# Order of a range check, a key transpose, a product block, a weight difference and three loads in a gated recurrence with a maxout layer

## The chip, the cores and the metric

The kernel runs on one core of one Trainium2 chip. The metric is the device time of one launch in microseconds. A profiled execution records every instruction of the five engines with its start and duration: TensorE (PE, with its weight loads as PEld), VectorE (DVE), ScalarE (ACT), GpSimd (POOL) and SyncE (SP), which here only issues DMAs. Each engine works through its own instructions in the order of the program and waits on semaphores.

## What is computed

There are two stages. The first is a recurrence for each of 4 batches and 8 heads over 768 steps, with states of 48 x 48. The second is a layer on the 3072 tokens of 384 features that the first one gives.

```python
f = 1.0 / (1.0 + np.exp(-f_logit))
for t in range(S):
    state = f[:, :, t, :, None] * state + np.einsum('bhd,bhe->bhde', k[:, :, t], v[:, :, t])
    y[:, :, t] = np.einsum('bhd,bhde->bhe', q[:, :, t], state)
# x is y with the heads of a token side by side
h = np.maximum(np.maximum(x @ w1, x @ w2), x @ w3)     # 384 -> 768
return h @ w_out                                        # 768 -> 384
```

The weights come as 64-bit floats. The kernel rounds them to 32 bits by integer and float operations on their two halves, and checks that their sizes lie in a range for which this rounding holds.

## The kernel before

**Units and groups.** The work is cut in 24 units of 128 tokens (64 steps of two batches). Four units make a group; group g is the layer's work on units 4g to 4g+3. A unit's part of the recurrence is: `sigmoids` (ACT, L305), `scan` (DVE: running products of the gates, L324), `after` (k times these, `kh`, L334), `before` (q times others, `qh`, L345), `carry` (L354), `keys` (transposes of `kh` into `ks`, on PE for units 4 and 5, and by 32 x 32 blocks on DVE from unit 6, L361 and L372), `pairs` (products of `kh` and `qh`, L389), `values` (L403), `sums` (L424) and `finish` (L496). `values` ends with a copy of one element on ACT, `seen` (L422), and the products of `finish` (L504) wait for it. From unit 6 on f, k and q are loaded two units at a time, in blocks of 32 rows: 8 DMAs for each of the three (L183), all issued by SP. `kt` and `qt` are the blocks transposed by DVE (L296), and from unit 6 the products `kh` (L340) and `qh` (L351) are made by POOL.

**Order.** The order is written out by hand (L992 onward). One loop over u from 4 to 23 (L1071) does, for each u, `pairs(u)`, `values(u-1)`, `sums(u-1)`, `finish(u-1)` and the preparation of unit u+1. Between them it calls `fill(ns)` (L967), which takes as many pieces of the layer's work from a generator as cost `ns` by an estimate. The generators yield after each block of products, so where a block stands in a generator decides which blocks lie between two steps of a unit. At u = 8 group 1 is put in the queue, at u = 12 group 2, and so on; the last group runs after the loop.

**The first group** (`ffn_first`, L797) runs plain products while the weights come in. Near its end it places w2 - w1 and w3 - w1 in another layout by DMAs inside the chip's memory (`place`, L454: 10 DMAs for each of the two, and 10 for a product of weights, w_lin). Then sums of placed weights are made (`mix_in`, L844, on POOL), and differences of w_out's quarters (`mix`, L588, on POOL). `mix(1)` overwrites a quarter of w_out, so the first group's products with w_out must have read it.

**Later groups** (`inputs_by_pairs`, L869) compute the two products of the layer's inputs by a scheme with fewer products: for each n of three, blocks named `start`, `plain`, `fifth`, `sixth`, `seventh`, `third` and `fourth`. Each call of `into` is two products of 256 columns (L881), which the profile shows as four records. Blocks accumulate in two kinds of PSUM banks: A[n] from a pool of two (named `p`) and B[n] from a pool of two (named `tr`). `plain(n)` fills B[n], and ACT copies it out (L889); `fifth(n)` writes B[n] anew, so it waits for that copy. `start(n)` fills A[n], copied by L895 into one buffer that POOL's `join(n)` (L899) reads; `sixth(n)` adds to A[n], copied by L909, and `seventh(n)` adds to it again, after that copy. `sixth` and `fifth` take sums of x made by POOL (`sums_of_x`, L856, five operations at L865); these need rows of x moved by `pack` (L519, DMAs at L524).

**The range check** of a piece of the weights (`check_range`, L272) is three steps on ACT: a size (L278) and two sums (L280), one piece for each unit from u = 10 on, and the rest after the loop.

**Names in the trace.** `tr` and `p` are the PSUM banks, `rest_bits` and `top_bits` also serve as buffers of the layer, `placed` holds the placed weights, `a` and `y` are the recurrence's banks. SPq means an issue by SP.

Of the kernel before, what the change touches and what calls it, by code (L numbers as in the profile page):

```python
# [55 lines left out]
def kernel(  # L56
# [15 lines left out]
    NU = B // 2 * (S // C)  # L72
# [5 lines left out]
    GRP = 4  # L78
# [11 lines left out]
    def fast():  # L90
        ctx = ExitStack()
        with ctx:
# [58 lines left out]
            BY_ROWS = 6  # L151
# [5 lines left out]
            one = (nc.sync, nc.sync)  # L157
# [590 lines left out]
            def store_late():  # L748
                while late:
                    store(*late.pop(0))  # L750
# [46 lines left out]
            def ffn_first(xT):  # L797
                hm = new_hm()
                steps = [(j, slice(n * HALF, (n + 1) * HALF)) for n in range(2) for j in range(J_HALF)]
                steps += [(j, slice(0, TOK)) for j in range(J_HALF, NJ)]  # L800
                n_step = 0
                for j, t in steps:
                    w = t.stop - t.start
                    for i in (1, 2):
                        p = yield from product(xT, j, i, t)
                        if i == 1:
                            nc.scalar.copy(hm[:, j, t], p)
                        else:
                            nc.vector.scalar_tensor_tensor(hm[:, j, t], hm[:, j, t], 0.0, p, op0=ALU.max, op1=ALU.max)
                        round_to(ROUNDED[n_step])  # L810
                        load_weights(2, rounded[0] - 1)
                        yield (1 if w == TOK else NK) * w * COLUMN
                        n_step += 1
                        if n_step in TURNED:
                            yield from turn(TURNED[n_step])
                for a in range(NK):
                    if a < 2:
                        for n in range(2 * NK + 2):
                            place(placed[a].bitcast(FP32), w_in[a + 1], n)
                    for cost in linear(a):  # L820
                        round_to(rounded[0] + 1)
                        yield cost
                for n in range(2 * NK + 2):
                    place(w_lin, w_nat, n)
                made = iter([lambda n=n: mix_in(n) for n in range(4)] + [lambda: mix(0)])
                for i in range(GRP):
                    for n, cost in enumerate(outputs(hm, xT, i)):
                        if i or n:
                            next(made, lambda: None)()
                        if i == GRP - 1 and n == 1 and 1 in packed:  # L830
                            sums_of_x(1)
                        if i == GRP - 1 and n == 2:
                            for k in range(1, 4):
                                mix(k)
                        yield cost

# [32 lines left out]
            def inputs_by_pairs(g, hm, xT):  # L869
# [37 lines left out]
                def sixth(n):  # L907
                    into(A[n], n, s2, t2)
                    nc.scalar.copy(out(n, 1), two(A[n]))  # L909
                    yield COST  # L910
# [29 lines left out]
                yield from plain(0)  # L940
                join(0)
                store_late()
                yield from sixth(0)
                yield from fifth(0)
                for n in range(1, NJ // 2):
                    yield from plain(n)
                    yield from seventh(n - 1)
                    yield from start(n)
                    join(n)
                    yield from third(n - 1)  # L950
                    yield from fifth(n)
                    yield from sixth(n)
                    yield from fourth(n - 1)
# [38 lines left out]
            with tc.manual_schedule():  # L992
# [78 lines left out]
                for u in range(GRP, NU):  # L1071
                    n = u + 1
                    part = EARLY if u < 2 * GRP else PART
                    if n == BY_ROWS:
                        scan(n)
                    fill(part)
                    keys(u)
                    keys_by_blocks(u, 2)
                    room_of_unit = room_of_pairs()
                    if u > GRP:  # L1080
                        values(u - 1)
                        sums(u - 1, room_of_unit)
                    pairs(u, room_of_unit)
                    if u > GRP:
                        finish(u - 1, xT)
                        if u % GRP == 3:
                            pack(0, 2, xT)
                        elif u % GRP == 0:
                            pack(3, 3, xT)
                    if u % GRP == 0:  # L1090
                        if u > GRP:
                            packed[u // GRP - 1] = xT
                            pending.append(ffn(u // GRP - 1, xT))
                        xT = x_tiles[u // GRP % 2]

                    if u + 2 <= BY_ROWS:
                        load(u + 2)
                    if BY_ROWS <= u + 3 < NU and u % 2:
                        load(u + 3, one, "fkq" if u % GRP == 1 else "f")
                    if u + 2 < NU:  # L1100
                        load_v(u + 2)
                    keys_by_blocks(u, 3)
                    if n < NU:
                        if n < BY_ROWS:
                            sigmoids(n)
                        if n != BY_ROWS:
                            scan(n)
                    check_range(u - CHECKS, 0)
                    fill(part)
                    if n < NU:  # L1110
                        after(n)
                        before(n)
                    fill(part)
                    if BY_ROWS < u + 2 < NU and u % GRP == 0:
                        load(u + 2, one, "k")
                    if n < NU:
                        carry(n)
                    else:
                        values(u)
                    check_range(u - CHECKS, 1)  # L1120
                    fill(part)
                    if BY_ROWS < u + 2 < NU and u % GRP == 0:
                        load(u + 2, one, "q")
                    if n == NU:
                        finish(u, xT)
                        pack(3, 3, xT, both)
                        packed[u // GRP] = xT
                    keys_by_blocks(n, 0)
                    fill(part - 1000 if u < 2 * GRP else part)
                    keys_by_blocks(n, 1)  # L1130
                    check_range(u - CHECKS, 2)
                    if u + 2 >= CHECKS:
                        check_load(u + 2 - CHECKS)
                    if BY_ROWS <= u + 2 < NU:
                        sigmoids(u + 2)
                fill(PART)
                pending.append(ffn(NU // GRP - 1, xT))
# [267 lines left out]
```

## Time and profile before

| what | us |
|---|---|
| median of 3 runs (lowest, highest) | 415.52 (415.32, 416.43) |
| the profiled execution's own time | 416.13 |
| its span, first to last instruction | 414.4 |
| PE busy in the span | 393.5 |
| DVE busy | 295.1 |
| POOL busy | 246.0 |
| ACT busy | 180.4 |

The span is the time from the first instruction to the last; what is left of the execution's time lies outside. Busy times are sums over the whole span, and the limits change on the way: weights arrive until some 60 us, the first group of the layer runs to 119 us, and groups 1 to 5 take the rest, group 5 without any unit beside it. In lines of the timeline the columns are the start in us, the duration, engine, source line, operation, what is written and read, the shapes and the number of records put together, and in brackets the engine's idle time before it and what ended that. A wait on several semaphores is put down to the one that came last. The granted TensorE clock is full over the whole span but its end (0.999 in the mean).

### The profile page before, as it was taken

The numbers are of one execution on the slowest core, as the hardware profiler recorded it, in microseconds if no ns is written. First come the engines' busy times: TensorE is split into PE (matmuls) and PEld (weight loads), VectorE is DVE, ScalarE is ACT, GpSimd is POOL, SyncE is SP. The second block draws the span as 40 slices with busy tenths as digits, with TensorE's granted clock in tenths as the row PEclk, the third lists the DMA queues.
The fourth block names the chain that finished last, engine by engine and source line by source line (L and its number), as shares of the span: only waits on it lengthen the run. The fifth ranks groups of instructions, "written<-read, shape, count | busy, mean of one in ns | idle before, by whom it ended". The sixth has DMA issues, their size and how long they took to land.

```text
span 414.4 us, 11516 instructions
## 1 busy us (share of the span) xinstructions
PE 393.5 (95%) x4598; PEld 331.8 (80%) x4598; DVE 295.1 (71%) x569; ACT 180.4 (44%) x430; POOL 246.0 (59%) x270
## 2 busy tenths in 40 slices
PE   5988999999999989999999999999999999999995
PEld 4766765556667878998889988899988889988994
DVE  6997896997785899898899997998995550002600
ACT  2488786421223522335532345532445424586110
POOL 2189694830969777567495296577377860435700
PEclk9999999999999999999999999999999999999999
DMA  8999886676356766277645276735374003542002
GB/s 168 238 271 272 246 228 90 85 139 161 84 103 99 122 108 124 57 96 114 114 123 109 43 112 85 148 87 89 60 144 110 2 17 88 133 133 72 0 21 62
DMA packets 181562, 47.21 MB, mean 114 GB/s; under 512 B 160448, under 2 KB 179200, under 8 KB 181504
## 3 DMA queue, kind: packets, MB, share of 16 engines
q1 hardware_dynamic: 178032, 45.62, 54.1%
q10 hardware_dynamic: 3472, 0.81, 0.9%
q8 instruction: 37, 0.61, 0.6%
q14 instruction: 21, 0.17, 0.1%
HBM read 37.75 MB, written 4.72 MB: 102 GB/s over the span
## 4 chain that ended last, share of the span: by engine, by line
PE 74%; SPq 6%; POOL 5%; DVE 5%; ACT 4%; issue 2%; DMA 2%; POOLq 0%
PE p L881 15%; PE p L636 14%; PE tr L881 12%; PE tr L636 10%; PE p L542 7%; PE p L568 3%; PE p L787 3%; PE y L415 2%; SPq L164 2%; SPq L174 2%; DVE ks L382 2%; PE y L504 2%; PE a L396 2%; PE a L433 2%; POOL w_in L258 1%
## 5 line engine op out<-in xcount | busy, mean ns | idle before, releaser
L382 DVE STREAM_TRANSPOSE ks<-kh 32x128 f32<-32x128 f32 x256 | 77.4, 302 | 13.4 <-POOL kh L340 9.4
L881 PE MATMUL tr<-xT,placed 128*128 128x256 f32 x300 | 71.5, 383 | 1.1 <-ACT hm L889 1.1
L881 PEld LDWEIGHTS tr<-xT,placed 128*128 128x128 f32 x300 | 56.0, 190 | 10.4 <-ACT hm L889 2.6
L881 PE MATMUL p<-xT,placed 128*128 128x256 f32 x180 | 44.8, 380 | 1.1 <-POOL xT L865 0.8
L339 POOL COPY ends<-r 128x8 f32<-128x8 f32 x24 | 8.8, 366 | 51.1 <-DVE r L329 51.1
L881 PEld LDWEIGHTS p<-xT,placed 128*128 128x128 f32 x180 | 33.9, 190 | 6.4 <-POOL xT L865 1.2
L542 PE MATMUL p<-xT,w_in 128*128 128x256 f32 (+1 forms) x108 | 34.0, 459 | 3.4 <-POOL w_in L756 1.9
L329 DVE TENSOR_TENSOR_SCAN r<-gate,from_one 128x520 f32<-128x520 f32 x24 | 32.5, 1354 | 6.1 <-ACT gate L308 2.8
L340 POOL TENSOR_TENSOR kh<-kt,r 128x512 f32<-128x512 f32 x18 | 30.9, 1715 | 7.6 <-DVE kt L296 7.6
L511 ACT COPY xT<-y 64x256 f32<-64x256 f32 (+1 forms) x60 | 22.1, 368 | 23.2 <-PE y L504 22.5
L347 DVE TENSOR_TENSOR_SCAN prod<-gate,from_inv 128x520 f32<-128x520 f32 x24 | 31.5, 1312 | 0.0
L608 POOL TENSOR_TENSOR w_in<-hm 128x256 f32<-128x256 f32 x15 | 11.1, 739 | 32.2 <-DVE hm L932 29.4
L644 DVE TENSOR_TENSOR o<-tr,w_in 128x384 f32<-128x384 f32 (+1 forms) x11 | 5.7, 521 | 34.3 <-PE tr L636 29.8
L881 PE MATMUL p<-w_in,placed 128*128 128x256 f32 x120 | 30.0, 379 | 0.0
L542 PEld LDWEIGHTS p<-xT,w_in 128*128 128x128 f32 x108 | 19.5, 190 | 12.6 <-issue 6.0
L924 DVE TENSOR_TENSOR hm<-tr,hm 128x512 f32<-128x512 f32 x15 | 10.3, 684 | 23.1 <-ACT raw L280 17.2
L258 POOL TENSOR_TENSOR w_in<-top_bits,rest_bits 128x384 uint32<-128x384 uint32 x18 | 21.9, 1223 | 7.2 <-DVE top_bits L252 3.8
L636 PE MATMUL p<-w_in,hm 128*128 128x192 f32 x120 | 25.3, 334 | 0.6 <-ACT w_in L641 0.6
L641 ACT COPY w_in<-p 128x384 f32<-128x384 f32 x15 | 7.2, 478 | 42.1 <-PE p L636 42.1
L280 ACT ACTIVATE raw<-top_bits 128x384 f32<-128x384 f32 x48 | 25.2, 526 | 0.4
L881 PEld LDWEIGHTS p<-w_in,placed 128*128 128x128 f32 x120 | 22.8, 190 | 3.1
L636 PE MATMUL tr<-w_out,w_in 128*128 128x192 f32 x120 | 24.4, 326 | 0.0
(156 smaller groups left out, 913.7 us busy)
## 6 DMA issues: line engine op xcount, KB each, us to landing
raw<-in_moe_w_dram SPq DMA_DIRECT2D x24, 384.0 KB, 4.3
v_ld<-in_v_dram SPq DMA_DIRECT2D x48, 96.0 KB, 3.3
placed<-in_moe_w_dram SPq DMA_DIRECT2D x12, 384.0 KB, 5.7
out_dram<-o SPq DMA_DIRECT2D x46, 96.0 KB, 2.2
placed<-in_moe_w_out_dram SPq DMA_DIRECT2D x6, 384.0 KB, 5.4
f_ld<-in_f_logit_dram SPq DMA_DIRECT2D x36, 64.0 KB, 2.6
k_ld<-in_k_dram SPq DMA_DIRECT2D x36, 64.0 KB, 2.5
q_ld<-in_q_dram SPq DMA_DIRECT2D x36, 64.0 KB, 2.5
```

Source lines behind the costliest of these rows:

```text
L258: nc.gpsimd.tensor_tensor(dst, by(top), by(rest), op=ALU.add)
L280: nc.scalar.activation(over, size, AF.Relu, scale=(-1 / HI_MIN, 1.0)[step - 1], bias=(1.0, -HI_END * (1 - 2.0 ** -24))[step - 1], accum_ou ...
L329: nc.vector.tensor_tensor_scan(r[:, 0:LEN][:, ::-1], flat(gate)[:, ::-1], flat(from_one)[:, ::-1], 1.0, op0=ALU.mult, op1=ALU.max)
L340: (nc.vector if u < BY_ROWS else nc.gpsimd).tensor_tensor(kh.rearrange("p h a t -> p a h t"), kt, by_batch(r[:, 1:LEN + 1].rearrange("p (x ...
L347: nc.vector.tensor_tensor_scan(flat(prod), flat(gate_tiles[u % 2]), flat(from_inv[u % 2]), 1.0, op0=ALU.mult, op1=ALU.max)
L382: nc.vector.transpose(ks[n * 32:(n + 1) * 32, :, par, e0:e0 + 32], kh[p0:p0 + 32, :, a, t0:t0 + 32])
L511: nc.scalar.copy(xT[o, :, t0 + a * C:t0 + (a + 1) * C], y[i, a, 0:HP * C].rearrange("p (h t) -> p h t", h=HP))
L542: nc.tensor.matmul(p if w < TOK else p.rearrange("p (two t) -> p two t", two=2), lhsT=w_in[i][:, kt, j * 128:(j + 1) * 128], rhs=x[:, t.st ...
L568: nc.tensor.matmul(p[:, 0:DM], lhsT=lhsT, rhs=rhs, start=(n == 0), stop=(n == NJ + NK - 1))
L636: nc.tensor.matmul(b[:, p * HD:(p + 1) * HD], lhsT=x, rhs=w, start=id(b) not in begun, stop=True, skip_group_check=True)
L787: nc.tensor.matmul(p[:, 0:DM], lhsT=w_in[0][:, a, j * 128:(j + 1) * 128], rhs=w_out[:, j, :], start=(j == 0), stop=(j == NJ - 1))
L881: nc.tensor.matmul(b[:, j * HALF:(j + 1) * HALF], lhsT=w[:, (2 * n + j) * 128:(2 * n + j + 1) * 128], rhs=x, start=begin and j == 0, stop= ...
```

## The change

Five edits, in the order of the diff:

- `mix(1)` is called before `sums_of_x(1)` in the first group's last outputs, and no longer behind it with `mix(2)` and `mix(3)`.
- `plain(1)` is yielded right behind `join(0)` and the late stores, before `sixth(0)` and `fifth(0)`; for n = 1 it is left out of its old place behind `fifth(0)`.
- `keys(u)` is called behind `values(u-1)` and `sums(u-1)`. It does anything for units 4 and 5 alone, and for unit 4 no `values` stands there.
- The loads of units 8 and 9 (both in one load, 24 DMAs): at u = 5 they are left out. At u = 6 f is loaded ahead of v(8), and k and q behind the third `fill` of the unit, which is behind the second placing in SP's order. `sigmoids(8)` is done at u = 7 ahead of `scan(8)`, and not at the end of u = 6.
- The first step of the range check, `check_range(u - 10, 0)`, stands behind the second `fill` of a unit and `after` and `before`, and not ahead of that `fill`.

DVE's instructions keep their order. On PE the four transposes of unit 5 and the blocks of `plain(1)` change places; on POOL one operation moves; on ACT L278, one L889 in each group, `seen` of unit 4 and the sigmoid of unit 8; on SP 24 loads.

```diff
-                        if i == GRP - 1 and n == 1 and 1 in packed:
-                            sums_of_x(1)
+                        if i == GRP - 1 and n == 1:
+                            mix(1)
+                            if 1 in packed:
+                                sums_of_x(1)
                         if i == GRP - 1 and n == 2:
-                            for k in range(1, 4):
+                            for k in range(2, 4):
                                 mix(k)
...
                 yield from plain(0)
                 join(0)
                 store_late()
+                yield from plain(1)
                 yield from sixth(0)
                 yield from fifth(0)
                 for n in range(1, NJ // 2):
-                    yield from plain(n)
+                    if n > 1:
+                        yield from plain(n)
                     yield from seventh(n - 1)
...
                     fill(part)
-                    keys(u)
                     keys_by_blocks(u, 2)
                     room_of_unit = room_of_pairs()
                     if u > GRP:
                         values(u - 1)
                         sums(u - 1, room_of_unit)
+                    keys(u)
                     pairs(u, room_of_unit)
...
-                    if BY_ROWS <= u + 3 < NU and u % 2:
+                    if u == BY_ROWS:
+                        load(u + 2, one, "f")
+                    elif u + 1 != BY_ROWS and BY_ROWS <= u + 3 < NU and u % 2:
                         load(u + 3, one, "fkq" if u % GRP == 1 else "f")
                     if u + 2 < NU:
                         load_v(u + 2)
                     keys_by_blocks(u, 3)
                     if n < NU:
-                        if n < BY_ROWS:
+                        if n < BY_ROWS or n == BY_ROWS + 2:
                             sigmoids(n)
                         if n != BY_ROWS:
                             scan(n)
-                    check_range(u - CHECKS, 0)
                     fill(part)
                     if n < NU:
                         after(n)
                         before(n)
+                    check_range(u - CHECKS, 0)
                     fill(part)
                     if BY_ROWS < u + 2 < NU and u % GRP == 0:
                         load(u + 2, one, "k")
+                    if u == BY_ROWS:
+                        load(u + 2, one, "kq")
...
-                    if BY_ROWS <= u + 2 < NU:
+                    if BY_ROWS <= u + 2 < NU and u != BY_ROWS:
                         sigmoids(u + 2)
```

`BY_ROWS` is 6, `GRP` is 4, `NU` is 24, `CHECKS` is 10, and n is u + 1 in the unit loop.

## Prediction

> **What bounds the kernel now.** I read the busy shares, then TensorE's own waits, then the timeline around each wait. The busy shares:
>
> ```profile
> PE 393.5 (95%) x4598; PEld 331.8 (80%) x4598; DVE 295.1 (71%) x569; ACT 180.4 (44%) x430; POOL 246.0 (59%) x270
> ```
>
> TensorE (PE) is busy for 95% of 414.4 us; only its waits, and what moves them, can give time. Those that matter here (waiting engine and line <- releaser: total us, times, longest):
>
> ```profile
> PE y L504 <- ACT seen L422: 2.2, 2, 1.5
> ...
> PE tr L881 <- ACT hm L889: 1.1, 3, 0.4
> PE p L881 <- POOL xT L865: 0.8, 1, 0.8
> ```
>
> By place these fall in two parts: a filling part up to 163 us, with five waits at 124.77 (0.82), 133.94 (0.27, on ScalarE's L895), 138.20 (0.33), 155.58 (1.53) and 163.41 (0.69); and a steady part in which PE is bound by itself but for three waits of 0.38 at 188.63, 247.56 and 306.49. Before the first of them PE is gapless from 80 to 120 us.
>
> The timeline says what the filling part hangs on (start, us, instruction, [idle before <- releaser]):
>
> ```profile
> 131.86 0.71 DVE L296 STREAM_TRANSPOSE kt<-k_ld 128x512 f32<-128x512 f32 x1 [4.43 <-DMA q_ld<-in_q_dram]
> ...
> 136.17 0.71 DVE L296 STREAM_TRANSPOSE qt<-q_ld 128x512 f32<-128x512 f32 x1 [1.81 <-DMA out_dram<-o]
> ...
> 136.96 1.18 POOL L351 TENSOR_TENSOR qh<-qt,prod 128x512 f32<-128x512 f32 x1 [1.47 <-DVE qt L296]
> ...
> 138.20 0.69 PE L396 MATMUL a<-qh,kh 48*64 48x64 f32 x32 [0.33 <-POOL qh L351]
> ```
>
> VectorE (DVE) idles 4.43 us for unit 10's k and 1.81 us for its q; q gives `qt`, `qt` gives `qh` on POOL, and `qh` releases `pairs(10)` at 138.20. From 136.17 DVE has work without a break until 163.4 (145 to 165 us: 19.11 of 20 us busy), and it ends the waits at 155.58 (a copy queued behind one that waits for DVE) and 163.41. So q of unit 10 sets when PE leaves the filling part. That q comes when SP gets to it. SP's queue:
>
> ```profile
> 71.02 5.32 SPq L183 DMA_DIRECT2D f_ld<-in_f_logit_dram  x8
> ...
> 87.21 1.32 SPq L458 DMA_DIRECT2D placed<-w_in  x2
> ...
> 95.24 1.84 SPq L458 DMA_DIRECT2D placed<-w_in  x2
> ...
> 129.86 4.15 SPq L183 DMA_DIRECT2D q_ld<-in_q_dram  x8
> ```
>
> SP issues end to end from 52 to 136 us, some 0.5 us for each DMA; it is an issue bound, without a wait of note.
>
> **What the skill says.** The Trainium skill, "DMA: Bandwidth & Descriptors", section "Issuing engines are not separate DMA queues", calls the sequencer's time to initiate a DMA usually small beside the DMA. Here it is not: 0.49 us each, back to back, is what makes q late. "PSUM — Partial Sum Buffer", section "Engine vs sequencer instructions": the queues of ScalarE, VectorE and GpSimd are strict FIFO, and matmuls start in program order. The trace agrees: the 0.14 us copy `seen` (L422) stands at 67.99 behind a 0.59 us copy that nobody waits for. "TensorE: Matmul & The Clock Gate", section "Single matmul latency", gives a single warm matmul a constant of some 166 ns beside its columns, which only a stream of them hides; the trace agrees in kind: a wait shown as 0.38 moves the next start by 0.53 (246.16 to 247.56 is 1.40, where the same four records elsewhere take 0.87), and the block after a wait lasts 1.13 in place of 1.03. So such a wait costs 0.53 + 0.10 = 0.63 us.
>
> **The change part by part.** Durations are of the profiled execution (span 414.4, 416.13 us in all, 0.6 above the median of 415.52); differences are carried to the median.
>
> 1. *Loads of units 8 and 9 behind the placing.* 24 DMAs leave 71.02 and go to two places. All they pass is on SP: 4 DMAs of v and 20 of placing. Nothing is added, so from 102.33 on SP's queue is the same in order and, as far as issue bounds it, in time. In between: v(7) at 71.0, first placing 72.4 to 78.8 (1.32 + 5.06), f 78.8 to 84.1, v(8) to 85.5, second placing 85.6 to 92.6, k to 96.8, q to 101.9. The sources are ready: the last of w2 - w1 ends on POOL at 61.8, of w3 - w1 on DVE at 67.75, and the raw words under both targets are read by 72.9. POOL's L850 waits 10.86 us for the second placing and starts at 102.67; it would start some 9.6 us earlier, at 93. That frees no PE: PE has no gap there. What is late instead: q of unit 8 lands at 101.9 + 2.5 = 104.4 (median landing of such a load 2.5), where `qt(8)` ran at 102.11. DVE then idled 2.99 us at 105.78 for `kh(8)`, which came late behind L850; now `kh(8)` is made at 101.1 and `qt(8)` ends at 105.1. `qh(8)` ends at 106.3, before 106.89; `pairs(8)` starts at 108.18. Cover 1.9 us (1.4 after part 2's gain); beyond that each us late would stall PE, which could still lose 2 us before 138.20. Cost 0. `sigmoids(8)` follows the copies that end at 96.68 on ScalarE, so the 0.62 us ends at 97.3; `gate(8)` ran at 97.59. Cost 0.
> 2. *Keys of unit 5 behind values and sums of 4.* `seen` goes ahead of the `ks` copy: it starts at 67.52 rather than 67.99, and L504, which stood for 0.71, starts 0.47 earlier. Four transposes only change places. Gain 0.47 at 68 us.
> 3. *mix(1) ahead of the five sums of x.* One L592 of 1.40 us moves into POOL's 3.74 us of idle before the first sum (123.18, held by the xT transfer). The products that read w_out ended near 117.2, so it doesn't wait. The sums end when they did, `join(0)` (L899) ends 1.47 earlier. If that idle were gone, the sums would be 1.40 later.
> 4. *plain(1) ahead of sixth(0).* Same 22 products and same bank count. In group 1 it puts 1.73 us of PE in front of the product that waits for POOL's sums: wait 0.82 (0.98 by starts) goes; with part 3 the 0.27 at 133.94 (0.43 by starts) nearly goes. Gain 1.4 at 134 us. The second bank of `tr` is free: in group 2 the addition that reads it ends at 183.6, and plain(1) would start after 187.
> 5. *Range check's first step later.* Read with part 4 in the steady part, where this stands (ScalarE, then PE, in group 3):
>
> ```profile
> 246.48 0.56 ACT L278 ACTIVATE top_bits<-raw 128x384 f32<-128x384 f32 x1
> 246.94 0.57 ACT L889 COPY hm<-tr 128x512 f32<-128x512 f32 x1
> 247.40 0.59 ACT L909 COPY hm<-p 128x512 f32<-128x512 f32 x1
> ```
>
> ```profile
> 246.16 1.03 PE L881 MATMUL p<-xT,placed 128*128 128x256 f32 x4
> 247.56 2.64 PE L881 MATMUL tr<-xT,placed 128*128 128x256 f32 x11 [0.38 <-ACT hm L889]
> ```
>
> fifth(0) may only write the bank when L889 has read it; one block of 0.87 covers that, and L278 pushes the copy past it. After the change fifth(0) has three blocks of cover. What is late next: seventh(0) must wait for L909, with fifth(0) alone as cover. ScalarE's order becomes L889, L889, L278, L909. Counted from the end of plain(1): L889 0.26 to 0.84 (a copy starts 0.26 behind its block, as 361.61 to 361.87 in the last group), L278 0.74 to 1.30, L909 1.20 to 1.79, PE at 1.83 in place of 1.73. That is a loss of 0.10 + 0.10 for a gain of 0.63: 0.43 net by this count; 0.37 if the copy starts 0.06 later. I take 0.4, three times: 1.2 us. Bounds per group: 0.53 (L278 costs nothing) and 0 (L909 as late as L889 was). In the last group L278 was not in the way (0.02 stall at 362.50): 0.
>
> **The sum.** Parts 2 to 4 bring PE to `pairs(10)` 1.9 us sooner, but q(10) lands when it did, DVE's 27 us behind it are in the same order, and PE waits 0.33 + 1.9 there. They give 0. Part 5: 3 x 0.4 = 1.2. Prediction 415.52 - 1.2 = 414.3 us.
>
> **Rivals.**
> - *The front gain lives.* SP's stretch has single issues of 1.0 to 1.5 us at 73.8, 83.3 and 95.9, some 2.5 us over their 0.5; if the new order avoids them, q(10) comes sooner and PE can follow by up to 1.9. Against: the number of DMAs is the same, and such issues recur every 10 to 19 DMAs. 415.5 - 1.2 - 1.9 = 412.4.
> - *The wait only changes hands.* seventh(0) waits as long for L909 as fifth(0) did for L889: 415.5. For it: one block of cover and L278 still ahead. Against: 0.43 more lateness is needed than I can count.
> - *SP slips, slower.* A load behind placing waits for its semaphore, the eighth DMA before it; 4.2 us of issue cover it, while placings land in up to 3.7 at the median. If that or an unlucky issue delays SP before q(10), every us goes one for one to the end. At the price of the longest single issue seen since 50 us (3.0): 415.5 - 1.2 + 3.0 = 417.3; it decides from 2.5 us.
>
> **Chances.** Mine 0.52, front gain 0.18, changed hands 0.15, slip 0.15. My own range is 413.6 to 415.0 (part 5 between 0.5 and 1.6 in all, q(10) within 0.4). Over all cases 412.3 to 416.6: it cuts the far half of the first rival and most of the slip. 0.3% is 1.25 us, about what a measurement here can tell from no change; my case lies on that edge, half of it counts as faster: 0.18 + 0.26 = 0.44 faster, 0.41 within, 0.15 slower.
>
> **What would show it.** Right: no PE wait at 124.77 and none on L889 in groups 2 to 4, small ones on L909; L850 near 93; the wait before `pairs(10)` near 2.2 and its start near 138.2. Wrong: `pairs(10)` moved by over 0.5, waits on L909 of 0.3 or more, or PE stalled at `pairs(8)`.

## The result, and the profile after

The changed kernel takes 413.75 us in the median of 20 runs (411.67 to 416.40), the kernel before 415.47 us in 20 runs beside it (413.06 to 416.66). The ratio is 0.9966, with a 95% interval of 0.9950 to 0.9982: 1.4 us less, between 0.7 and 2.1. Predicted were 414.3 us.

The profiled execution of the changed kernel took 413.13 us with a span of 411.4 us, 3.0 us less than that of before. The two profiles so differ by about twice as much as the runs do (1.4 us by the ratio, 1.7 by the medians), and the experiments have to say which part of the 3.0 us belongs to the change. In the changed kernel the lines from L832 to L942 have moved down by two: L881 is now L883, L889 is L891, L909 is L911.

The busy shares of the page after:

```profile
PE 392.9 (96%) x4598; PEld 331.9 (81%) x4598; DVE 294.6 (72%) x569; ACT 180.8 (44%) x430; POOL 245.7 (60%) x270
```

PE's busy time is the same within 0.6 us; what went is idle time. PE's waits after (engine, line <- releaser: total us, times, longest):

```profile
PE y L504 <- ACT seen L422: 1.5, 1, 1.5
PE a L396 <- POOL qh L351: 0.8, 1, 0.8
...
PE p L636 <- DVE hm L933: 0.7, 1, 0.7
```

The three waits on L889 have no successor, neither on L891 nor on L911. The wait for `xT` at 124.77, the one for `rest_bits` at 133.94 and the first of the two for `seen` are gone; the one ahead of `pairs(10)` has grown from 0.33 to 0.83 us, and the two behind it are as they were (1.53 and 0.69 before). The timeline there, DVE, POOL and PE:

```profile
134.46 0.71 DVE L296 STREAM_TRANSPOSE qt<-q_ld 128x512 f32<-128x512 f32 x1 [2.39 <-DMA out_dram<-o]
...
135.25 1.18 POOL L351 TENSOR_TENSOR qh<-qt,prod 128x512 f32<-128x512 f32 x1 [2.20 <-PE y L415]
...
136.48 0.69 PE L396 MATMUL a<-qh,kh 48*64 48x64 f32 x32 [0.83 <-POOL qh L351]
```

The chain from q by `qt` and `qh` to `pairs(10)` is the same, but all of it stands 1.7 us earlier. (The profile puts the wait of `qh` down to PE's L415, which ends within 0.03 us of `qt` here; in e6 below L415 ends 4.4 us ahead of `qh`, and the time from q's landing to `pairs(10)` is the same.) So does q in SP's queue, which is issued from 128.14 us where it was from 129.86:

```profile
78.11 5.78 SPq L183 DMA_DIRECT2D f_ld<-in_f_logit_dram  x8
...
128.14 4.15 SPq L183 DMA_DIRECT2D q_ld<-in_q_dram  x8
```

In the steady part, group 3, ScalarE and then PE:

```profile
245.94 0.59 ACT L891 COPY hm<-tr 128x512 f32<-128x512 f32 x1 [1.02 <-PE tr L883]
246.42 0.57 ACT L278 ACTIVATE top_bits<-raw 128x384 f32<-128x384 f32 x1
246.88 0.58 ACT L911 COPY hm<-p 128x512 f32<-128x512 f32 x1
```

```profile
246.60 1.03 PE L883 MATMUL tr<-xT,placed 128*128 128x256 f32 x4
247.61 1.10 PE L883 MATMUL p<-w_in,placed 128*128 128x256 f32 x4
```

The order on ScalarE is the predicted one: L891, L278, L911. fifth(0) starts at 246.60 without a wait; seventh(0), at 247.61, comes 1.01 us behind it where 0.87 is its natural distance. That is 0.14 late, and the block behind it is another 0.07 late.

Split at the start of `pairs(10)`, the difference of the two profiled spans (3.0 us) is 1.72 us ahead of it and 1.28 us behind it. Behind it stand the three distances that hold the removed waits (`pairs(13)` to `pairs(14)`, 17 to 18 and 21 to 22): 14.94, 14.93 and 14.93 us before, 14.50, 14.51 and 14.50 after, 1.29 us in all. The steady part is so accounted for; the 1.72 us ahead of `pairs(10)` are the question.

### The profile page after: what moved, and what is told of

It reads as the page before. It is cut to its first block, busy times and chain, and to the rows that moved or that the text cites. A ratio compares the mean times of both kernels' runs of the same rounds, so it can differ in the third digit from the quotient of the medians.

```text
span 411.4 us, 11515 instructions
## 1 busy us (share of the span) xinstructions
PE 392.9 (96%) x4598; PEld 331.9 (81%) x4598; DVE 294.6 (72%) x569; ACT 180.8 (44%) x430; POOL 245.7 (60%) x270
## 4 chain that ended last, share of the span: by engine, by line
PE 85%; DVE 6%; POOL 3%; issue 2%; DMA 1%; ACT 1%; SPq 0%; DVEq 0%; POOLq 0%
PE p L883 17%; PE tr L883 15%; PE p L636 14%; PE tr L636 10%; PE p L542 7%; PE p L568 6%; PE p L787 3%; PE y L415 3%; PE a L396 3%; PE a L433 2%; PE y L504 2%; DVE ks L382 2%; PE tr L291 1%; POOL w_in L258 1%; DMA f_ld<-in_f_logit_dram 1%
## 5 line engine op out<-in xcount | busy, mean ns | idle before, releaser
L382 DVE STREAM_TRANSPOSE ks<-kh 32x128 f32<-32x128 f32 x256 | 77.3, 302 | 10.3 <-POOL kh L340 6.3
L883 PE MATMUL tr<-xT,placed 128*128 128x256 f32 x300 | 71.1, 382 | 0.0
L883 PEld LDWEIGHTS tr<-xT,placed 128*128 128x128 f32 x300 | 56.3, 190 | 8.0
L883 PE MATMUL p<-xT,placed 128*128 128x256 f32 x180 | 44.6, 379 | 0.0
L339 POOL COPY ends<-r 128x8 f32<-128x8 f32 x24 | 6.9, 288 | 56.9 <-DVE r L329 56.9
L340 POOL TENSOR_TENSOR kh<-kt,r 128x512 f32<-128x512 f32 x18 | 33.4, 1855 | 10.6 <-DVE kt L296 10.6
L883 PEld LDWEIGHTS p<-xT,placed 128*128 128x128 f32 x180 | 34.1, 190 | 4.7
L329 DVE TENSOR_TENSOR_SCAN r<-gate,from_one 128x520 f32<-128x520 f32 x24 | 33.4, 1391 | 5.9 <-ACT gate L308 2.8
L347 DVE TENSOR_TENSOR_SCAN prod<-gate,from_inv 128x520 f32<-128x520 f32 x24 | 30.5, 1269 | 0.0
L883 PE MATMUL p<-w_in,placed 128*128 128x256 f32 x120 | 30.4, 382 | 0.0
L883 PEld LDWEIGHTS p<-w_in,placed 128*128 128x128 f32 x120 | 22.4, 190 | 4.4 <-issue 1.3
```

The source lines that it names most:

```text
L329: nc.vector.tensor_tensor_scan(r[:, 0:LEN][:, ::-1], flat(gate)[:, ::-1], flat(from_one)[:, ::-1], 1.0, op0=ALU.mult, op1=ALU.max)
L340: (nc.vector if u < BY_ROWS else nc.gpsimd).tensor_tensor(kh.rearrange("p h a t -> p a h t"), kt, by_batch(r[:, 1:LEN + 1].rearrange("p (x ...
L347: nc.vector.tensor_tensor_scan(flat(prod), flat(gate_tiles[u % 2]), flat(from_inv[u % 2]), 1.0, op0=ALU.mult, op1=ALU.max)
L382: nc.vector.transpose(ks[n * 32:(n + 1) * 32, :, par, e0:e0 + 32], kh[p0:p0 + 32, :, a, t0:t0 + 32])
L883: nc.tensor.matmul(b[:, j * HALF:(j + 1) * HALF], lhsT=w[:, (2 * n + j) * 128:(2 * n + j + 1) * 128], rhs=x, start=begin and j == 0, stop= ...
```

## The experiments

The theory is that SP's issuing sets when q of unit 10 lands and with it `pairs(10)` and all that follows, so that of the five edits only what shortens the steady part changes the time, and that the 1.72 us are scatter of SP's own pace. The rivals are that one of the other edits brings q(10) in sooner (the loads), or that PE and the copies set `pairs(10)` and the front edits earn their 1.9 us.

In the table "q(10) in" is the landing of its last DMA, "behind" is the time from the start of `pairs(10)` to the end of the span; both are from the profiled execution. Median and ratio are from all runs of that kernel and of the kernel before beside it (its medians there are 415.43, 415.45 and 415.69 us).

| kernel | q(10) in | pairs(10) | behind | median us | ratio (95%) |
|---|---|---|---|---|---|
| before | 136.05 | 138.20 | 276.2 | 415.47 | 1 |
| whole change | 134.33 | 136.48 | 274.9 | 413.75 | 0.9966 (0.9950–0.9982) |
| e1: parts 4, 5 | 135.93 | 138.08 | 274.9 | 413.67 | 0.9953 (0.9939–0.9968) |
| e2: part 1 | 134.61 | 136.77 | 276.2 | 414.87 | 0.9999 (0.9979–1.0018) |
| e3: parts 2, 3 | 135.89 | 138.04 | 276.2 | 415.51 | 1.0006 (0.9984–1.0027) |
| e4: part 5 | 134.78 | 136.93 | 275.3 | 413.91 | 0.9966 (0.9949–0.9983) |
| e5: part 4 | 134.79 | 136.96 | 274.7 | 414.18 | 0.9972 (0.9955–0.9989) |
| e6: whole, 8 more loads | 139.26 | 141.40 | 274.8 | 418.90 | 1.0080 (1.0060–1.0100) |
| e7: whole, stores on ACT | 153.96 | 156.16 | 274.9 | 432.66 | 1.0407 (1.0382–1.0433) |
| e8: e7, and f(10) on ACT | 145.79 | 153.02 | 271.9 | 426.71 | 1.0262 (1.0238–1.0286) |
| e9: whole, stores deferred | 129.73 | 135.98 | 271.9 | 410.21 | 0.9890 (0.9856–0.9923) |
| e10: before, stores deferred | not in the trace | 137.12 | 274.2 | 412.24 | 0.9914 (0.9887–0.9941) |

### e1 to e4: the parts alone

e1, plain(1) and the range check (parts 4 and 5):

```diff
+                yield from plain(1)
                 yield from sixth(0)
...
-                    yield from plain(n)
+                    if n > 1:
+                        yield from plain(n)
...
-                    check_range(u - CHECKS, 0)
                     fill(part)
                     if n < NU:
                         after(n)
                         before(n)
+                    check_range(u - CHECKS, 0)
```

> Only the plain block and the range check are moved; loads, keys and the weight difference stay as before. My theory (all the steady gain is here, and q of unit 10 sets the rest): the three waits of fifth(0) on L889 go, the distance from pairs(13) to pairs(14) falls from 14.94 to 14.50 us, the wait of sixth(0) at 124.8 goes but pairs(10) starts when q of unit 10 has landed, as before; total 1.3 us less than before (0.4 to 2.2 with the spread of SP's issue). Rival (the gain of the whole change comes from the loads' new place, which makes q of unit 10 earlier): total within 0.6 of 1.3 less, but pairs(10) 1.7 us later than in the whole change and the whole change about 1 us faster than this.

e2, the loads of units 8 and 9 and the sigmoid of unit 8 (part 1):

```diff
+                    if u == BY_ROWS:
+                        load(u + 2, one, "f")
-                    if BY_ROWS <= u + 3 < NU and u % 2:
+                    elif u + 1 != BY_ROWS and BY_ROWS <= u + 3 < NU and u % 2:
...
-                        if n < BY_ROWS:
+                        if n < BY_ROWS or n == BY_ROWS + 2:
                             sigmoids(n)
...
+                    if u == BY_ROWS:
+                        load(u + 2, one, "kq")
...
-                    if BY_ROWS <= u + 2 < NU:
+                    if BY_ROWS <= u + 2 < NU and u != BY_ROWS:
                         sigmoids(u + 2)
```

> Only the loads of units 8 and 9 and the sigmoid of unit 8 are moved. My theory (SP's issues are only put in another order): q of unit 10 is issued at 129.9 within 1 us either way, the three waits on L889 stay, total within 0.6 us of before; L850 starts near 93 us. Rival (the new order saves SP time): q of unit 10 is issued 1 us or more earlier, as in the profiled execution of the whole change (128.1), and the total falls by as much, 1.0 to 1.7 us.

e3, keys of unit 5 and mix(1) (parts 2 and 3):

```diff
-                        if i == GRP - 1 and n == 1 and 1 in packed:
-                            sums_of_x(1)
+                        if i == GRP - 1 and n == 1:
+                            mix(1)
+                            if 1 in packed:
+                                sums_of_x(1)
                         if i == GRP - 1 and n == 2:
-                            for k in range(1, 4):
+                            for k in range(2, 4):
                                 mix(k)
...
-                    keys(u)
...
                         sums(u - 1, room_of_unit)
+                    keys(u)
```

> Only the keys of unit 5 and the one weight difference are moved. My theory: the wait of L504 at 68 us goes (0.5 us), the wait of sixth(0) on the sums of x grows by as much or pairs(10) waits longer, and pairs(10) does not move against the landing of q of unit 10: total within 0.5 us of before. Rival (front gains live): 0.5 to 1.0 us less than before.

e4, the range check alone (part 5):

```diff
-                    check_range(u - CHECKS, 0)
                     fill(part)
                     if n < NU:
                         after(n)
                         before(n)
+                    check_range(u - CHECKS, 0)
```

> Only the first step of the range check is moved. My theory (fifth(0) needs L889 alone out of the way; one block of cover is just enough when ScalarE is free): the three waits of 0.38 shrink to less than 0.1, the distance from pairs(13) to pairs(14) falls from 14.94 to about 14.45, total 1.5 us less than before, so this edit alone does the steady part and plain(1) adds nothing to it. Rival (the plain block's cover is what removes the wait): the distance stays above 14.7 and the total within 0.6 us of before.

Measured: e1 has all of the gain (0.9953, 2.0 us less, between 1.3 and 2.5), and e2 and e3 have none (0.9999 and 1.0006). In e1 and the whole change the time behind `pairs(10)` is 1.3 us shorter, in e2 and e3 it is that of before. So the gain lies in the steady part, and the loads, the keys and mix(1) give nothing that these runs can see; their intervals leave room for some 1 us either way.

Yet e2's profile shows q(10) 1.44 us earlier than before, as the whole change does, while its times are unchanged. And e4, which touches no load at all, has it 1.27 us earlier. The place of q(10) in a single profile therefore says little on the edit. The trace shows how it scatters. From the last issue of L218 to the first DMA of q(10), SP issues 115 DMAs in each of the seven kernels from before to e5, one behind the other. That takes between 77.0 us (whole change) and 78.1 us (before), and it starts between 51.0 and 52.7 us. Most of these DMAs take 0.49 to 0.6 us; 8 to 10 of them in each profile take over 0.8 us, up to 3.2 us, and are 7.4 to 8.7 us above 0.55 us each in all. These long ones come at nearly the same times in all seven: one near 55 us, which is the longest, and one each at 66.9 to 67.5, 82.4 to 83.7, 95.7 to 96.3 and 108.7 to 109.2 us, whatever DMA is issued there. So a new order does not avoid them; their cause stays open. For the pair of profiles shown first, the start of this stretch is 0.63 us earlier after and its length 1.09 us shorter, which is the 1.72 us.

A small effect of the loads' new order is not excluded. The two profiles that have it show the earliest q(10) of the seven (134.33 and 134.61 us, the others 134.78 to 136.05), though the stretch is no shorter in e2 (77.3 us) than in e3 (77.2), which has the old order. e2's times bound such an effect to some 0.9 us.

What is constant is the link: from the landing of q(10) to `pairs(10)` it is 2.14 to 2.17 us in before, in the whole change and in e1 to e6. PE itself is never far behind: it waited 0.19 us ahead of `pairs(10)` in e2, and in e5 the profile shows no wait there. A q(10) that came sooner still would no longer be what `pairs(10)` waits for.

e3 shows two smaller things. Without the 0.71 us at 68 us PE came to `pairs(8)` early enough to wait 0.27 us for `qh(8)`, and `pairs(7)` to `pairs(8)` took 14.26 us in place of 13.82: with the loads in their old place nearly all of part 2's 0.47 us was already lost there. In the whole change `qh(8)` ended at 105.36, and `pairs(8)` started at 107.49 without a wait. And e3 shows a gain being swallowed: q(10) lands as late as before, the waits at 124.77 and 133.94 are gone, and PE is ready for `pairs(10)` at 137.20 in place of 137.87 us, but it waits 0.84 us there in place of 0.33. In e1, which lacks mix(1), the wait at 124.77 is gone and the one on L895 (133.83 there) has grown from 0.27 to 1.07 us: plain(1) alone brings PE to `pairs(10)` hardly sooner (137.76).

e4 came out as its theory said, where the prediction had read parts 4 and 5 as one cure: the range check's move alone takes the distance 13 to 14 from 14.94 to 14.49 us, as much as with plain(1) (14.50). ScalarE in group 3 of e4:

```profile
247.52 0.56 ACT L278 ACTIVATE top_bits<-raw 128x384 f32<-128x384 f32 x1
248.77 0.59 ACT L889 COPY hm<-tr 128x512 f32<-128x512 f32 x1 [0.68 <-PE tr L881]
```

With plain(1) in its old place, L278 falls behind the copies that PE waits for, with room on both sides. (Its time behind `pairs(10)` is 0.4 us longer than e1's: the granted TensorE clock was 0.66 from 155 to 160 us in that profile, and `pairs(11)` to `pairs(12)` took 18.43 us in place of 17.98.)

### e5: plain(1) alone

```diff
+                yield from plain(1)
                 yield from sixth(0)
...
-                    yield from plain(n)
+                    if n > 1:
+                        yield from plain(n)
```

> The kernel before with plain(1) moved ahead of sixth(0), and the range check left where it was (its first step between the copies of fifth(0)). Theory A, that the copies of fifth(0) are late only because plain(1) stood one place too late, so that one more block of TensorE work ahead of seventh(0) covers them: the distance from one pairs to the next of the next group goes from 14.93 to about 14.50 us, as with both edits, and the total falls by 3 x 0.43 = 1.3 us (ratio 0.997). Theory B, that the range check's copy between the copies of fifth(0) is what makes them late wherever plain(1) stands: the distance stays at 14.9 us, and the total is that of before (ratio 1.000).

Measured: theory A, and a little more. The three distances are 14.43 us each, 0.50 less than before, and the time 0.9972 of before. ScalarE in group 3 of e5:

```profile
244.74 0.55 ACT L278 ACTIVATE top_bits<-raw 128x384 f32<-128x384 f32 x1
245.19 0.57 ACT L889 COPY hm<-tr 128x512 f32<-128x512 f32 x1
246.34 0.59 ACT L889 COPY hm<-tr 128x512 f32<-128x512 f32 x1 [0.58 <-PE tr L881]
247.20 0.59 ACT L909 COPY hm<-p 128x512 f32<-128x512 f32 x1 [0.28 <-PE p L881]
```

L278 still stands ahead of the first copy and makes it as late as before, but fifth(0) now comes three blocks behind plain(0) and doesn't feel it; and L909 starts at 247.20, 0.03 us behind the end of its product on PE (246.14 + 1.03), with nothing ahead of it for 0.28 us. So each of the two edits alone removes the wait on L889. Together they are worth no more than one (0.43, 0.44 and 0.50 us), since the moved check then falls between the copies of plain(1) and of sixth(0) and makes seventh(0) late by 0.14 (0.06 in e5).

### e6: SP made later

```diff
                     check_range(u - CHECKS, 0)
+                    if u == 8:
+                        load(8, one, "f")
                     fill(part)
```

> The whole change, and in unit 8 one more load of f of unit 8 (8 DMAs, issued by SP ahead of those of k and q of unit 10; it brings again what is there already). At 0.52 us an issue that is about 4.2 us more on SP ahead of q(10). Theory, that the landing of q(10), and so SP's issuing, sets the start of pairs(10) and with it the end: q(10) lands, pairs(10) starts and the kernel ends about 4.2 us later than with the whole change (3.5 to 4.8), which is 417 to 418.5 us, ratio to before about 1.007. Rival, that TensorE or the copies set it and the landing only happens to come at about the same time: less than 1 us against the whole change.

The time grew to 418.90 us, ratio 1.0080. In the profile q(10) lands 4.93 us later than in the whole change and `pairs(10)` starts 4.92 us later. PE's timeline in e6:

```profile
141.40 1.13 PE L396 MATMUL a<-qh,kh 48*64 48x64 f32 x32 [5.16 <-POOL qh L351]
```

The wait grew from 0.83 to 5.16 us, and the time behind it is the same 274.8 us (274.9 in the whole change): what SP loses ahead of q(10) goes one for one to the end. The expected 4.2 us became 4.9 in the profile because the stretch also began 0.96 us later there; the scatter again.

The 1.13 us of `pairs(10)`, 0.69 in the whole change, are another matter. The granted clock was halved during and behind this wait (the columns are those of e9 below; the clock is the third number from the end):

```profile
139.00:145.00 6.00, 3.60 (x68) 3.19 (x69) 5.44 (x12) 1.10 (x3) 4.41 (x4) 0.50 0.79 148
```

From `pairs(10)` to `pairs(11)` e6 takes 17.15 us in place of 15.19. None of this reached `pairs(12)`, as the next distance is 15.99 in place of 17.98 us, with the wait for `seen` gone. So PE's own speed did not set the stretch to `pairs(12)`.

### e7 and e8: SP made earlier, by moving issues to ACT

e7 sends the first group's eight output stores by ACT; e8 does that and issues f of unit 10 by ACT too.

```diff
-            def store(u, o):
+            def store(u, o, queue=nc.sync):
...
-                    nc.sync.dma_start(out=out[t0:t0 + C, :], in_=o[a * C:(a + 1) * C, :])
+                    queue.dma_start(out=out[t0:t0 + C, :], in_=o[a * C:(a + 1) * C, :])
...
-                            store(i, o)
+                            store(i, o, nc.scalar)
```

> The whole change, and the 8 output stores of the first group issued by ACT instead of SP; six of them stand ahead of q(10) in SP's queue and cost it about 3.6 us there. Theory, that SP's issuing sets pairs(10): q(10) lands about 3.6 us earlier, pairs(10) starts about 0.8 us earlier, as early as TensorE comes to it, and the waits behind it (1.5 us at L504 and 0.7 us at the products of p, both for what follows from late q and f) shrink too; 2 to 3 us less than the whole change, ratio to before about 0.991. Rival, that TensorE's own work or a copy sets it, or that ACT's issuing of the stores makes its copies late by as much: the same time as the whole change within 0.5 us, ratio about 0.9966.

e8 has these lines and two more:

```diff
-                                    nc.sync.dma_start(
+                                    queues[0].dma_start(
...
-                        load(u + 3, one, "fkq" if u % GRP == 1 else "f")
+                        load(u + 3, act if u == 7 else one, "fkq" if u % GRP == 1 else "f")
```

> As the run with the stores on ACT, and the 8 DMAs of f of unit 10 are issued by ACT as well: about 8 us off SP's queue ahead of q(10). Theory, that SP's issuing bounds the stretch to pairs(12): all three waits of TensorE there (0.83, 1.5 and 0.7 us) are nearly gone, up to 3 us less than the whole change, ratio to before 0.989 to 0.991. Rival, that ACT's 16 issues at about 0.55 us make its copies late, and TensorE waits for these instead: no better than the run with the stores alone, or worse than the whole change.

Both expectations failed: 432.66 and 426.71 us, slower by 17 and 11 us. The profile of e7 says why; first SP's own largest wait between 60 and 150 us and PE's, then SP's timeline:

```profile
SPq L465 <- DMA out_dram<-o: 15.1, 2, 10.5
```

```profile
PE a L396 <- POOL qh L351: 16.8, 2, 15.6
```

```profile
88.38 21.55 SPq L465 DMA_DIRECT2D placed<-w_in  x8
```

The eight loads of the second placing, 5.0 us in the whole change, took 21.55 us: SP stood for the output stores, though the placing touches nothing of them. The stores stood in ACT's queue behind copies that wait for PE; the first four were issued at 99.28 and 105.08 us:

```profile
99.28 1.20 ACTq L560 DMA_DIRECT2D out_dram<-o  x2
105.08 1.12 ACTq L560 DMA_DIRECT2D out_dram<-o  x2
```

The placing followed only as these landed, and SP came to k and q of unit 8 only at 109.98, in place of 91.89. `pairs(8)` so waited 15.6 us. The trace shows the reason. It names the semaphore that each DMA counts on and waits for: in this kernel SP's and ACT's DMAs take the same eight in turn, and each DMA waits until the one that had its semaphore before has landed. The second, third and fourth store landed at 102.08, 107.17 and 107.81 us, and the DMAs of the placing that took over their semaphores were issued at 102.10, 107.19 and 107.82. So a DMA on one engine waited for one on another without sharing data.

So these two kernels do not test the theory in the part that they were made for. They show one thing of use: in e8 SP was ahead of PE behind that stall (q(10) in at 145.79, `pairs(10)` at 153.02 without a wait), neither the wait for `seen` nor that for `hm` is left, and the time behind `pairs(10)` fell to 271.9 us, 3.1 less than in the whole change.

### e9 and e10: SP made earlier, without another engine

Here the stores stay on SP, but are kept back until the loads of unit 12 are issued; e9 is the whole change with this, e10 the kernel before with this.

```diff
+            late, held = [], [True]
+
             def store(u, o):
+                if held[0]:
+                    late.append((u, o))
+                    return
...
                         load(u + 3, one, "fkq" if u % GRP == 1 else "f")
+                        if u == 2 * GRP + 1:
+                            held[0] = False
+                            for i, o in late:
+                                store(i, o)
```

> The whole change, and the 8 output stores of the first group kept back on SP until the loads of unit 12 are issued, so that six of them no longer stand ahead of q(10) and all eight no longer ahead of f, k and q of unit 12. No DMA is moved to another engine. Theory, that SP's issuing sets the start of pairs(10) and the two waits behind it: q(10) lands about 3.7 us earlier, TensorE's wait of 0.83 us ahead of pairs(10) goes, those of 1.5 us (L504) and 0.7 us (products of p) shrink; 1 to 3 us less than the whole change (ratio to before 0.990 to 0.994). Rival, that TensorE's or the copies' own work sets the end there: the same as the whole change within 0.5 us (ratio 0.9966).

> The kernel before, with the same 8 stores kept back until the loads of unit 12 are issued. It is the partner of the run above: the difference of the two is what the whole change is worth where SP no longer sets pairs(10). Theory, that the gain of keys, mix and plain(1) in the front (1.9 us by the prediction) was only swallowed by the wait for q(10): the difference of the two totals grows from 1.7 to about 2.5 to 3.2 us. Rival, that these edits bring nothing even then, since the waits they remove were due to late loads as well: the difference is 1.3 us, the gain of the steady part alone.

e9 takes 410.21 us, 0.9890 of before and 3.5 us less than the whole change by the medians (3.2 by the ratios): the best kernel of this study. q(10) lands at 129.73 us, 4.6 us sooner than in the whole change (about 3.7 were expected) and 6.25 us ahead of `pairs(10)`, where the link was 2.15. Busy times by stretch (window, its length, then PE's busy time and records, PEld, DVE, ACT, POOL, PE's clock, DMA share, GB/s), of the whole change and then of e9:

```profile
100.00:140.00 40.00, 39.17 (x510) 29.26 (x509) 30.26 (x62) 12.39 (x28) 31.08 (x26) 1.00 0.61 106
140.00:180.00 40.00, 37.75 (x438) 34.65 (x438) 36.96 (x76) 14.21 (x37) 26.55 (x30) 1.00 0.55 95
```

```profile
100.00:140.00 40.00, 40.00 (x514) 29.87 (x514) 32.01 (x72) 12.93 (x29) 34.74 (x31) 1.00 0.61 96
140.00:180.00 40.00, 40.00 (x516) 37.22 (x515) 36.90 (x77) 14.40 (x38) 26.89 (x31) 1.00 0.68 129
```

PE is busy for the whole of both stretches in e9: the wait ahead of `pairs(10)`, the one of 1.54 us for `seen` and the one of 0.70 us for `hm` are all gone. From `pairs(10)` to `pairs(12)` it takes 30.13 us in place of 33.17. Of these 3.04 us, 1.75 are the wait for `seen` by starts, and 1.25 that for `hm`, whose next block also ran slower (1.03 us to the following start in place of 0.65). All three waits hung on SP's issuing.

e10 tells what the change is worth where q(10) no longer sets `pairs(10)` (`qh` ends there 2.1 us ahead of it). It takes 412.24 us. So the whole change is worth 2.0 us by the medians of e9 and e10, 1.0 by the ratios and 3.5 in the two profiles; with six runs on each side the times do not decide between the rival's 1.3 and the theory's 2.5 to 3.2. The traces say where the difference lies:

- From `pairs(4)` to `pairs(8)`, where the keys stand, e9 is 0.68 us shorter. 0.20 of this is lost by e10 at `pairs(8)`, which waits there for a late `qh(8)`.
- From `pairs(8)` to `pairs(10)`, where mix(1) and plain(1) were to earn 1.4 us, e10 takes 28.13 us and e9 27.99: 0.14 us.
- From `pairs(10)` to `pairs(12)` it is 1.02 us, as e10 keeps a wait of 0.47 us for `hm`. Whether an edit removes that one, or SP's pace (q(10) is issued at 122.99 us in e9 and at 126.21 in e10), was not separated.
- Behind `pairs(12)` it is 1.33 us, the steady part.

The waits at 124.77 and 133.94 hung on SP as well. `sums_of_x` starts when the rows of x have landed that `pack` moves by SP's queue (L524), and `join(0)`, with L895 behind it, follows these sums on POOL. The sums in before, in e3 and in e10:

```profile
123.18 1.53 POOL L865 TENSOR_TENSOR xT<-xT 128x256 f32<-128x256 f32 x2 [3.74 <-DMA xT<-xT]
```

```profile
123.04 1.53 POOL L867 TENSOR_TENSOR xT<-xT 128x256 f32<-128x256 f32 x2 [0.47 <-DMA xT<-xT]
```

```profile
121.62 1.54 POOL L870 TENSOR_TENSOR xT<-xT 128x256 f32<-128x256 f32 x2
```

The rows landed at 123.02 us in before, and at 121.28, 121.74 and 121.46 in e2, e4 and e10. These three have neither mix(1) nor plain(1) moved, and neither wait is in their profiles. In e3 the rows landed as late as before (122.88), and with mix(1) moved neither wait is left, in part because PE came 0.57 us later. So there are two ways to nothing: with SP late the edits take the waits away and `pairs(10)` takes the gain back; with SP early the waits are not there.

## Why the prediction was right, and where it was not

- **What bounds the kernel.** Right: SP's issuing sets q(10), and q(10) sets `pairs(10)`. e6 shows it from one side (4.93 us later in, 4.92 us later out), e9 from the other. One issue is short beside the landing of its DMA (0.49 against 2.5 us in the prediction's own numbers); what makes q late is that 115 stand in a row, at 0.67 us each with the long ones.
- **Part 1, the loads: cost 0.** Right: 0.9999, between 0.9979 and 1.0018, in e2. The placed weights' L850 (now L852) started at 92.56 us, said was 93; `qh(8)` ended at 105.36, said was 106.3; PE did not stall at `pairs(8)`.
- **Part 2, keys: 0.47 us, swallowed.** Right in size: `pairs(4)` to `pairs(8)` went from 55.15 to 54.67 us. Right that it doesn't reach the end: e3's ratio is 1.0006. In e3 it did not even reach `pairs(8)`.
- **Parts 3 and 4 in the front: 1.4 us, swallowed.** The zero was right, and e3 shows the swallowing that was given as its reason. What the prediction left out is that the two waits hang on SP too. It read the first as held by the transfer of x, but took it as fixed; e2, e4 and e10 have neither wait with rows of x that land 1.3 to 1.7 us sooner. So the 1.4 us are no reserve that a faster SP would set free: in e9 against e10 they are 0.14.
- **Part 5: 0.43 us a group by count, 0.4 taken, times three.** Right in size: 0.43, three times. The loss at seventh(0) was counted as 0.10 + 0.10 and measured as 0.14 + 0.07. The attribution fell short: the wait on L889 has two independent cures. The range check alone gives 0.44 (e4), plain(1) alone 0.50 (e5), both 0.43. The upper bound of 0.53 per group, "L278 costs nothing", is nearly what e5 measured, with L278 left where it was.
- **The sum.** 1.2 us against a measured 1.4 by the ratio, 1.7 in the medians and 1.3 in the traces behind `pairs(10)`. The rest is within the runs' uncertainty of 0.7 us.
- **The sign that failed.** `pairs(10)` was to start near 138.2 with a wait near 2.2 before it, and a shift of over 0.5 was to count as wrong. It moved by 1.72, and the wait was 0.83. By its own rule the profile spoke against the forecast, and for the first rival, the front gain that lives. The step that failed is "q(10) within 0.4", that one profile of each kernel would show its place to half a microsecond. It scatters by 1.7 us (134.33 to 136.05 in the seven profiles from before to e5) with the same 115 DMAs ahead of it. e2 shows it 1.44 us early at an unchanged time. The medians differ by 1.7, not by 3.0.
- **The rivals.** "The wait only changes hands" is out: no wait on L911. "SP slips" has its price confirmed by e6, one for one, but the moved loads did not make SP slip. "The front gain lives" is out as an effect of the edits, beyond the 1 us or so that the intervals of e2 and e3 leave open.

## What to carry to other kernels

Where one queue's issuing sets the end of a stretch, the small waits ahead of that point can be its shadows, as two were here: ask of each what it hangs on before giving it to the edit that stands next to it, and shorten that queue first. Here eight stores that nobody waits for, put behind the urgent loads, were worth 3.6 us (e10 by its ratio), where the five edits of order brought 1.4. Compare such places in several profiles before reading a shift of 1 to 2 us as an effect, and move work to another engine's queue only after asking what waits for its completion there.

## What the runs showed that was not expected

- SP's issues are not even: of 115 in a row, 8 to 10 take 0.8 to 3.2 us where most take 0.49 to 0.6, and what they take above 0.55 us each is 7.4 to 8.7 us of 77 to 78. They come at nearly the same times in every profile. Here, where SP sets `pairs(10)`, they pass into the time.
- A DMA on SP waited 10.5 us at a stretch for a store that stood in ACT's queue and shared no data with it, but had its semaphore before it (e7).
- After a wait of 0.70 us in the whole change a block took 1.03 us by starts in place of 0.65, at a granted clock of 1.00. A wait can so cost more than the profile puts down to it: 0.70 shown was 1.25 in the end. The slow products behind the wait of 5.16 us in e6 are no such case, as the granted clock was 0.50 there.
